# Gram products in four array tiles, T's second layout made on PE, and the first group's 16-to-32 merge as PE products, under a new hand-written order

## The chip, the cores and the metric

The kernel runs on one core of one Trainium2 chip. The metric is the device time of one execution in microseconds (us), lower is better. Before the change the median of three runs is 352.01 us (350.1 to 353.36).

## What is computed

A gated delta rule (linear attention with a correcting state) for 4 x 8 heads, 768 steps, head dimension 48, and behind it a gated convolution layer over the 384 joined features. All data are float32 (the three layer weights arrive as float64 and are converted on the chip).

```python
for t in range(S):
    kt, vt, bt = (k_n[:, :, t], v[:, :, t], beta[:, :, t, None])       # k_n: k divided by its norm
    y[:, :, t] = np.einsum('bhd,bhde->bhe', q[:, :, t], state)
    v_old = np.einsum('bhde,bhd->bhe', state, kt)
    state = state + bt[:, :, :, None] * np.einsum('bhd,bhe->bhde', kt, vt - v_old)
...
for k in range(K):                                                     # K = 5 taps, per feature
    gate_pre += conv_w[k][None, None, :] * xp[:, k:k + S, :]
gate = 1.0 / (1.0 + np.exp(-gate_pre))
val = x @ w_val
return (gate * val @ w_out).astype(np.float32)
```

## The kernel before

The 768 steps are cut into 12 chunks of 64, and two chunks form a **group** (6 groups). Inside a chunk the recursion is solved at once: with the Gram matrix of the keys (64 x 64 for each of the 32 heads, 16 pairs of heads side by side), a triangular inverse T turns values into corrected values; only the 48 x 48 state is handed from chunk to chunk.

**Per group, `prep(g)`.** Four loads `KQ` (keys and queries of half a chunk's heads; three buffers). `gram` on PE (TensorE) writes the Gram products of four pairs into a PSUM bank, key against key and query, with a contraction of 48: one head of a pair lies in partitions 64 to 111 and writes output rows 0 to 63, the other lies in 0 to 47 and writes rows 64 to 127. So two 64 x 64 tiles of the array work at once. ACT (ScalarE) copies the bank to `GL`, then the diagonal blocks of 32 to `D1`. DVE (VectorE) transposes them in 32 x 32 blocks (`TL`; this row opens a group's work on DVE), works out the coefficients (`coef`, 18 small rows), and inverts each block of 32: `row` up to size 8, `mergez8` and `merget8` from 8 to 16, and **`zmul`/`zred`/`tmul`/`tred` from 16 to 32**. Part of those products runs on POOL (GpSimd): two of eight in the first group (whose six others are on DVE), four in the later ones. `D1` is their scratch, so the next group's diagonal copies wait until they are done. Last, DVE transposes the result **twice** (`trans_out`): into `TTR`, and in the other layout into `TNA`. From 32 to 64 the step is on PE: `lev1` (tile `z`), a copy to `ZS`, `lev2` (tile `t`, with `TNA` as the stationary side), and a copy into `BD`, the full T of a chunk.

**Per chunk, `chain(ch)`**: products `e` (state by keys), `u` (T by values) and `SPS` (state update), with `eevac` on DVE between `e` and `u` and copies on ACT; then `y`, whose result goes to `YS` and `X`, and six small DMAs (`X<-YS`) that lay the features out.

**Per chunk, `moe(ch)`**: two of five taps as PE products (`conv`), three on DVE (`tap`, in PSUM), the sigmoid on ACT, `val` on PE, `gate` on DVE, `out` on PE, and the stores.

PSUM has 8 banks: 2 for the state, 3 in a pool "c" (chain, conv, y), 3 in a pool "w" (gram, z, t, val, out).

**Order.** Each helper is an entry of a plan with its engine. The table `ORDER` lists the entries by number, and each engine runs its own entries in that order, strictly one after another, waiting on semaphores; entries of -1 are `keep_warm` products of zeros on PE. SP (SyncE) issues all loads in its own part of that order. The weights pass through two staging slots: a load, ACT and DVE rows on the bits (`f64_bits`, four rows on DVE), a copy, and two POOL rows (`f64_join`); the next load of a slot waits for them.

## Time and profile before

| | |
|---|---|
| median of 3 runs | 352.01 us (350.1 to 353.36) |
| the profiled execution | 352.4 us, span 350.7 us |
| PE busy | 318.4 us (91%), of which products of zeros (L758) 32.9 us |
| DVE busy | 260.8 us (74%) |
| ACT busy | 194.3 us (55%) |
| POOL busy | 123.0 us (35%) |
| mean granted PE clock | 0.946 |

The profiled execution is 0.1% above the median. A row of a view names the line, the engine, the operation, the tile written and the tiles read, with shapes. PE records a float32 product twice, so 32 products of `gram` appear as 64 records; matmuls overlap in the array, so a record's own duration is longer than the step from one to the next. `PEclk` is the granted clock of PE as a share of full speed.

### The profile page before, as it was taken

Reading aid. Unit: us, or ns where it says so; the run is one execution under the profiler, and the core shown is the slowest. Engines: PE = TensorE matmul, PEld = TensorE weight load, DVE = VectorE, ACT = ScalarE, POOL = GpSimd, SP = SyncE. Lnnn points to the kernel's source line nnn. Section 1 sums busy time; section 2 is a strip of 40 time slices with the busy share of each in tenths; the row PEclk is TensorE's granted clock in tenths of the full one; section 3 lists DMA queues with packets and bytes.
Section 4 is the critical chain, followed back from the end, with each engine's and each line's share of the span. In section 5 each row is a group of like instructions: output and inputs, shape, how many; then the busy total and the mean of one; then the engine's idle time right before and its main releaser. Section 6 shows DMA issues by size and latency. Waiting matters only on the chain.

```text
span 350.7 us, 13815 instructions
## 1 busy us (share of the span) xinstructions
PE 318.4 (91%) x5998; PEld 262.1 (75%) x5998; DVE 260.8 (74%) x565; ACT 194.3 (55%) x428; POOL 123.0 (35%) x92
## 2 busy tenths in 40 slices
PE   8769997689299799999799999999988999999994
PEld 5768997689288687878668778777677787687872
DVE  5038999999789876999956999789885689612550
ACT  6643400898149853379764797447973421974221
POOL 6425047034891026512068400545204564000000
PEclk9985899668769999999999999999999999999999
DMA  7999711036274534144574435135253332101122
GB/s 201 249 269 277 190 52 47 7 104 187 67 170 133 151 110 118 32 141 126 140 200 119 136 99 152 50 85 158 56 152 104 80 78 49 38 15 36 36 45 45
DMA packets 20283, 39.47 MB, mean 113 GB/s; under 512 B 8112, under 2 KB 11312, under 8 KB 20224
## 3 DMA queue, kind: packets, MB, share of 16 engines
q1 hardware_dynamic: 20224, 38.60, 41.5%
q8 instruction: 47, 0.77, 0.9%
q14 instruction: 12, 0.10, 0.1%
HBM read 32.69 MB, written 4.72 MB: 107 GB/s over the span
## 4 chain that ended last, share of the span: by engine, by line
PE 62%; DVE 21%; ACT 6%; DMA 5%; issue 3%; POOL 1%; SPq 0%; ACTq 0%; DVEq 0%
PE val L704 14%; PE out L715 12%; PE conv L689 9%; PE gram L351 6%; DMA KQ<-in_kq_dram 5%; PE e L570 5%; PE u L570 3%; PE SPS L570 3%; PE y L638 3%; PE y L640 2%; DVE PR L426 2%; DVE TT__83 L433 2%; PE z L450 2%; PE t L470 2%; ACT D L214 2%
## 5 line engine op out<-in xcount | busy, mean ns | idle before, releaser
L694 DVE SCALAR_TENSOR_TENSOR conv<-X,CW,conv 128x256 f32<-128x256 f32 x108 | 48.5, 486 | 19.7 <-PE conv L689 12.8
L351 PE MATMUL gram<-KQ 48*64 48x128 f32 x768 | 54.0, 295 | 6.1 <-DMA KQ<-in_kq_dram 5.6
L704 PE MATMUL val<-X,WV 128*128 128x256 f32 x216 | 53.4, 388 | 1.3 <-ACT GL L214 1.3
L351 PEld LDWEIGHTS gram<-KQ 48*64 48x64 f32 x768 | 47.7, 147 | 8.5 <-issue 3.5
L715 PE MATMUL out<-WO,GT 128*128 128x384 f32 x144 | 50.3, 490 | 0.0
L704 PEld LDWEIGHTS val<-X,WV 128*128 128x128 f32 x216 | 39.5, 189 | 8.5 <-ACT GL L214 1.4
L214 ACT ACTIVATE GL<-gram 128x512 f32<-128x512 f32 x48 | 28.1, 596 | 23.1 <-PE gram L351 22.7
L689 PE MATMUL conv<-X,DW 128*128 128x256 f32 x144 | 37.9, 399 | 0.5 <-DMA X<-YS 0.5
L715 PEld LDWEIGHTS out<-WO,GT 128*128 128x128 f32 x144 | 26.8, 189 | 15.0 <-issue 0.2
L570 PE MATMUL u<-VT,BD 64*64 64x48 f32 x768 | 31.1, 230 | 7.2 <-DVE VT L622 6.2
L570 PEld LDWEIGHTS u<-VT,BD 64*64 64x64 f32 x768 | 27.3, 144 | 10.7 <-issue 8.7
L548 POOL TENSOR_SCALAR_AFFINE_SELECT AQ<-GL 64x1024 f32<-64x1024 f32 x24 | 28.3, 1180 | 16.5 <-PE y L638 12.2
L214 ACT ACTIVATE D<-GL 32x512 f32<-32x512 f32 (+1 forms) x36 | 22.7, 631 | 19.7 <-DVE TT__83 L433 19.1
L758 PEld LDWEIGHTS SPS<-ZW 128*128 128x128 f32 x242 | 31.3, 210 | 2.8 <-issue 2.7
L758 PE MATMUL SPS<-ZW 128*128 128x128 f32 x242 | 32.9, 298 | 0.0
L708 DVE TENSOR_TENSOR GT<-val,GT 128x256 f32<-128x256 f32 x36 | 15.0, 420 | 20.8 <-PE val L704 18.8
L689 PEld LDWEIGHTS conv<-X,DW 128*128 128x128 f32 x144 | 26.2, 193 | 5.1 <-issue 0.6
L342 POOL TENSOR_TENSOR VT<-VT,NRM 128x768 f32<-128x768 f32 x12 | 17.7, 1477 | 35.1 <-DMA VT<-in_vt_dram 27.7
L638 PE MATMUL y<-AQ,US 112*64 112x64 f32 x384 | 29.1, 233 | 0.0
L638 PEld LDWEIGHTS y<-AQ,US 112*64 112x64 f32 x384 | 25.9, 146 | 3.6 <-issue 2.2
L698 ACT ACTIVATE GT<-conv 128x256 f32<-128x256 f32 x36 | 13.4, 387 | 27.1 <-DVE conv L694 27.0
L640 PE MATMUL y<-AQ,US 128*48 128x64 f32 x384 | 28.0, 230 | 0.0
(97 smaller groups left out, 591.2 us busy)
## 6 DMA issues: line engine op xcount, KB each, us to landing
KQ<-in_kq_dram SPq DMA_DIRECT2D x24, 448.0 KB, 4.7
KF<-in_kf_dram SPq DMA_DIRECT2D x11, 448.0 KB, 3.9
VT<-in_vt_dram SPq DMA_DIRECT2D x12, 384.0 KB, 4.1
AQ<-in_qf_dram SPq DMA_DIRECT2D x24, 192.0 KB, 3.6
KT<-in_kt_dram SPq DMA_DIRECT2D x12, 384.0 KB, 3.5
out_dram<-OS SPq DMA_DIRECT2D x48, 96.0 KB, 2.2
AQ<-in_w_val_dram SPq DMA_DIRECT2D x3, 384.0 KB, 11.0
AQ<-in_w_out_dram SPq DMA_DIRECT2D x3, 384.0 KB, 12.7
```

The source lines that it names most:

```text
L214: A.activation(out=out, in_=in_, func=AF.Copy, **kw)
L342: G.tensor_tensor(out=VT[c], in0=VT[c], in1=NRM[:, c * NP:(c + 1) * NP].unsqueeze(2).to_broadcast([128, NP, D]), op=ALU.mult)
L351: PE.matmul(p[64 * a:64 * a + 64, 128 * j:128 * (j + 1)], x[:, 0:C], x, start=True, stop=True)
L548: G.affine_select(out=AQ[c][r0:r0 + 64, j], in_=GL[r0:r0 + 64, c * NP:(c + 1) * NP, 64:128], pattern=[[0, NP], [1, C]], compare_op=ALU.is_ ...
L570: return lambda: PE.matmul(*a, stop=True, **k)
L638: PE.matmul(p[0:64, C * j:C * j + C], US[ch % 3][0:112, 0, h, D * j:D * j + 64], AQ[c][0:112, 0, pp, :], start=True, stop=True)
L640: PE.matmul(p[64:112, C * j:C * j + C], us[:, 1, h, j, :], AQ[c][:, 1, pp, :], start=True, stop=True)
L689: PE.matmul(p[:, 0:B * C].rearrange("p (b t) -> p b t", t=C), DW[:, m, i, :], x[:, m, :, k:k + C], start=(i == 0), stop=(i == len(PTAPS) - 1))
L694: V.scalar_tensor_tensor(out=p, in0=x[:, m, :, k:k + C], scalar=CW[:, m, k:k + 1], in1=p, op0=ALU.mult, op1=ALU.add)
L704: PE.matmul(p[:, 0:B * C].rearrange("p (b t) -> p b t", t=C), WV[:, k, 128 * m:128 * m + 128], xs[:, k], start=(k == 0), stop=(k == NKT - 1))
L715: PE.matmul(bank["o", ch, i][:, 0:DM], GT[k][:, 2 * i:2 * i + 2, :].rearrange("p b t -> p (b t)"), WO[:, k, :], start=(k == 0), stop=(k == ...
L758: PE.matmul(SPS[0][:, 384:512], ZW, ZW, start=False, stop=True, skip_group_check=True)
```

## The change

1. **Gram in four tiles.** The host swaps the two partition halves for the upper four pairs of each `KQ` load. `gram` now takes a whole load at once, eight pairs into two banks, and goes round the four 64 x 64 tiles. There are 24 calls of 16 products instead of 48 of 8; each holds two of the three "w" banks. The number of products (384) and their size are the same.
2. **T's layout on PE.** The second DVE transpose goes in groups 1 to 5. Instead `lev0` multiplies `TTR` by the identity `EYE` (tile `n`, 32 products a chunk), and ACT copies it to `TN`. `z`, `n` and `t` now lie in four strips of 32 partitions that match, so `zevac` is one copy of 128 partitions instead of four of 32; `lev2` uses four tiles of the array on its diagonal.
3. **The first group's merge on PE** (`MERGE = (0,)`): `TTR` and `TNA` are transposed with the two blocks of 16 still apart; `mergew` (128 products of 32x16), a DVE row `mergew_evac` into `WI`, `mergeq` (128 more) and an ACT copy into `TTR` supply the missing corner. The 16 rows of zmul to tred of group 0 (14 on DVE, 2 on POOL) go. The later groups keep theirs.
4. Small: `halves` (16 short POOL rows at the start, for the constants `IDH` and `ML`); `PTAPS` unchanged, the new branches on it don't act.
5. **A new `ORDER`**: every engine's rows move; `keep_warm` goes from 121 products to 53.

```diff
+MERGE = (0,)
 ORDER = [
-    1, 4, 8, 2, 16, 110, 5, 160, 3, 65, 162, 6, 70, 9, 10, 7, 11, 12, 13, 161, 0, 14, 75, 15, 17, 24, 64, 18, 19,
+    -3, 66, 9, 17, 67, 71, 76, 151, 10, 68, 11, 12, 13, 14, 15, 72, 18, 2, 0, 6, 16, 19, 20, 21, 22, 25, 81, 69, 70,
...
+        def gram_bank(c, h):
+            bank["g", g, c, 2 * h] = wps("gram")
+
         def gram(c, h):
-            p = bank["g", g, c, h] = wps("gram")
-            kq_ = KQ[(4 * g + 2 * c + h // 2) % 3]
+            bank["g", g, c, 2 * h + 1] = wps("gram")
+            kq_ = KQ[(4 * g + 2 * c + h) % 3]
             for j in range(QB):
-                for a, r in ((0, slice(64, 112)), (1, slice(0, D))):
-                    x = kq_[r, QB * (h % 2) + j, :]
-                    PE.matmul(p[64 * a:64 * a + 64, 128 * j:128 * (j + 1)], x[:, 0:C], x, start=True, stop=True)
+                for a in range(2):
+                    for s in range(2):
+                        r = 64 * (a ^ s ^ 1)
+                        x = kq_[r:r + D, QB * s + j, :]
+                        PE.matmul(bank["g", g, c, 2 * h + s][64 * a:64 * a + 64, 128 * j:128 * (j + 1)], x[:, 0:C], x,
+                                  start=True, stop=True)
...
+        def mergew(c):
+            for u in range(c * NP, (c + 1) * NP):
+                for r in range(0, 128, 32):
+                    PE.matmul(bank["mw", g][r:r + 32, 16 * u:16 * u + 16], GL[r:r + 32, u, r % 64:r % 64 + 32],
+                              TTR[r:r + 32, u, 16:32], start=True, stop=True, tile_position=(r, r))
+        def mergew_evac():
+            V.scalar_tensor_tensor(
+                out=WI, in0=bank["mw", g].rearrange("p (u x) -> p u x", x=16), scalar=ML[:, 0:1],
+                in1=IDH.unsqueeze(1).to_broadcast([128, NU, 16]), op0=ALU.mult, op1=ALU.add)
+        def mergeq(c):
...
+                    PE.matmul(bank["mq", g][r:r + 32, 16 * u:16 * u + 16], TNA[r:r + 32, u, :], WI[r:r + 32, u, :],
+                              start=True, stop=True, tile_position=(r, r))
+        def mergeq_evac():
+            copy(A, TTR[:, :, 16:32], bank["mq", g].rearrange("p (u x) -> p u x", x=16))
+        def lev0(c):
+            p = bank["n", g, c] = wps("n")
+            for pp in range(NP):
                 u, x = c * NP + pp, 32 * (pp // 2)
                 for r in (0, 64):
-                    to = r + 32 * (pp % 2)
+                    to = 64 * (pp % 2) + r // 2
+                    PE.matmul(p[to:to + 32, x:x + 32], TTR[r:r + 32, u, :], EYE[r:r + 32, r:r + 32],
+                              start=True, stop=True, tile_position=(r, to))
+        def nevac(c):
+            copy(A, TN, bank["n", g, c][:, 0:256].rearrange("p (u x) -> p u x", x=32))
...
-                    PE.matmul(p[to:to + 32, x:x + 32], TNA[r:r + 32, u, :], ZS[r:r + 32, pp, :],
-                              start=True, stop=True, tile_position=(r, to))
+                    PE.matmul(p[to:to + 32, 32 * x:32 * x + 32], TN[to:to + 32, x, :], ZS[to:to + 32, x, :],
+                              start=True, stop=True, tile_position=(to, to))
...
+        if g in MERGE:
+            add("DVE", 1.15, trans_out, (0,), r=["TT"], w=["TTR"])
+            add("DVE", 1.15, trans_out, (1,), r=["TT"], w=["TNA"], kind="trans_nat")
...
-        add("DVE", 1.15, trans_out, (1,), r=["TT"], w=["TNA"])
...
+    kq[:, :, 0:D, QB:], kq[:, :, 64:112, QB:] = kq[:, :, 64:112, QB:].copy(), kq[:, :, 0:D, QB:].copy()
```

The new order shows at three places. First SP, which issues the loads, from the start of the program. Before, the fourth `KQ` load (the second time `KQ0` stands) is the 13th load; the rows are loads 2 to 13:

```order
L219 DMA AQ1_79<-in_w_val_dram 128x768
L219 DMA VT1_75<-in_vt_dram 128x768
L219 DMA KQ0_67<-in_kq_dram 112x1024
L219 DMA AQ0_78<-in_qf_dram 48x1024
L219 DMA KQ1_68<-in_kq_dram 112x1024
L219 DMA BE_108<-in_beta_dram 128x192
L219 DMA AQ0_78<-in_qf_dram 48x1024
L219 DMA KQ2_69<-in_kq_dram 112x1024
L219 DMA AQ1_79<-in_w_val_dram 128x768
L219 DMA KF1_77<-in_kf_dram 112x1024
L219 DMA VT0_74<-in_vt_dram 128x768
L219 DMA KQ0_67<-in_kq_dram 112x1024
```

With the change, SP's loads 1 to 10:

```order
L223 DMA KQ0_67<-in_kq_dram 112x1024
L223 DMA AQ1_79<-in_conv_w_dram 128x30
L223 DMA AQ1_79<-in_w_val_dram 128x768
L223 DMA KQ1_68<-in_kq_dram 112x1024
L223 DMA KQ2_69<-in_kq_dram 112x1024
L223 DMA AQ1_79<-in_w_val_dram 128x768
L223 DMA KQ0_67<-in_kq_dram 112x1024
L223 DMA VT1_75<-in_vt_dram 128x768
L223 DMA BE_108<-in_beta_dram 128x192
L223 DMA AQ1_79<-in_w_val_dram 128x768
```

The fourth `KQ` is now the seventh load, and the loads of `qf`, `kf` and the other values stand behind the third part of `w_val`.

Second DVE, where group 0's inverse ends. Before, the last rows of the merge (L426 and L433), then both transposes, then the first row of group 1 (L364); the rows on AQ1 belong to the weights:

```order
L426 TENSOR_TENSOR PR<-ZT,TT__83 128x512
L433 TENSOR_REDUCE TT__83<-PR 128x16x4
L426 TENSOR_TENSOR PR<-ZT,TT__83 128x768
L433 TENSOR_REDUCE TT__83<-PR 128x16x4
L273 TENSOR_SCALAR AQ_79<-AQ_79 128x384
L433 TENSOR_REDUCE TT__83<-D_86 128x16x4
L275 TENSOR_SCALAR AQ_79<-AQ_79 128x384
L438 STREAM_TRANSPOSE TTR<-TT__83 128x32x32
L440 STREAM_TRANSPOSE TNA<-TT__83 128x32x32
L277 SCALAR_TENSOR_TENSOR AQ_79<-AQ_79 128x384
L364 STREAM_TRANSPOSE TLP<-D_86 128x32x32
```

With the change the same place (L422 and L427 are the last rows from 8 to 16; ROOT, NRM and QUOT are coefficients, of group 1 here):

```order
L422 TENSOR_TENSOR PR<-ZT,TT__83 128x256 x2
L427 TENSOR_REDUCE TT__83<-PR 128x2x8x4
L341 TENSOR_TENSOR ROOT<-SS,ROOT 128x32
L293 TENSOR_SCALAR X_99<-X_99 128x384
L343 TENSOR_SCALAR ROOT<-ROOT 128x32
L457 STREAM_TRANSPOSE TTR<-TT__83 128x32x32
L345 STREAM_TRANSPOSE NRM_110<-ROOT 128x32
L459 STREAM_TRANSPOSE TNA<-TT__83 128x32x32
L347 TENSOR_TENSOR QUOT<-ROOT 128x32
L349 RECIPROCAL QUOT<-QUOT 128x32
L470 SCALAR_TENSOR_TENSOR WI<-mw,ML,IDH 128x512
```

Group 1's first transpose and most of its coefficients have moved ahead of group 0's `TTR`, and the 16-to-32 rows of group 0 are gone.

Third PE between the last early `gram` and the first chunk's `u`. Before:

```order
L351 MATMUL gram<-KQ_68 64x128 x16
L758 MATMUL SPS_120<-ZW 128x128 x73
L450 MATMUL z<-TTR,GL_80 32x32 x32
L351 MATMUL gram<-KQ_69 64x128 x16
L351 MATMUL gram<-KQ_67 64x128 x16
L470 MATMUL t_675<-ZS,TNA 32x32 x32
```

With the change:

```order
L369 MATMUL gram<-KQ_68 64x128 x16
L824 MATMUL SPS_124<-ZW 128x128 x48
L466 MATMUL mw<-TTR,GL_80 32x16 x128
L824 MATMUL SPS_124<-ZW 128x128 x2
L479 MATMUL mq<-WI,TNA 32x16 x128
L491 MATMUL n<-EYE,TTR 32x32 x32
L503 MATMUL z<-TTR,GL_80 32x32 x32
L369 MATMUL gram<-KQ_69 64x128 x16
L519 MATMUL t_918<-ZS,TN 32x32 x32
```

Fewer products of zeros stand ahead, and `mw`, `mq` and `n` stand between `TTR` and `z`.

## The prediction

> **What bounds the kernel now.** I read first the busy time of the engines by stage, cut at rows of DVE that the whole program waits for: the first transpose of group 0 (26.58), the ends of `TTR` of groups 0, 1 and 5 (64.24, 108.58, 298.25), and the last copy of `out` (346.2). Columns: stage, length, busy us of PE, its weight loads, DVE, ACT, POOL, then granted clock.

> ```profile
> 0.00:26.58 26.58, 20.10 (x184) 16.33 (x184) 8.31 (x25) 15.51 (x30) 11.63 (x17) 0.94 0.95 240
> 26.58:64.24 37.66, 32.74 (x302) 31.11 (x302) 36.01 (x68) 8.75 (x16) 15.06 (x8) 0.86 0.48 130
> 64.24:108.58 44.34, 36.81 (x892) 33.39 (x892) 39.61 (x73) 30.33 (x64) 25.09 (x17) 0.73 0.41 112
> 108.58:298.25 189.67, 181.41 (x3823) 145.62 (x3824) 158.06 (x362) 115.86 (x264) 71.00 (x49) 1.00 0.42 113
> 298.25:346.20 47.95, 47.31 (x799) 35.63 (x797) 18.78 (x40) 23.36 (x57) 0.22 (x1) 1.00 0.14 31
> ```

> Three regimes. Until 26.58 the DMA engines set the pace (share 0.95). Until 108.58 it is DVE (75.6 of 82.0 us; PE's busy time there holds most of its products of zeros). From 108.58 it is PE: 8.3 us idle of 189.67, then 0.6 of 47.95, while DVE has 31.6 us to spare. So work taken from DVE shortens the second regime in full and the third only through waits; work taken from PE shortens the third.

> **First regime.** The chain of waits and the rows of time show what starts DVE's row at 26.58.

> ```profile
> 10.99 0.31 SPq L219 DMA_DIRECT2D KQ<-in_kq_dram  x1
> 21.85 2.10 PE L351 MATMUL gram<-KQ 48*64 48x128 f32 x32 [2.73 <-DMA KQ<-in_kq_dram]
> 24.04 0.36 DVE L273 TENSOR_SCALAR AQ<-AQ 128x384 f32<-128x384 f32 x1 [4.06 <-ACT AQ L271]
> 24.61 1.93 ACT L214 ACTIVATE D<-GL 128x512 f32<-128x512 f32 x3
> 26.58 2.08 DVE L364 STREAM_TRANSPOSE TLP<-D 128x1024 f32<-128x1024 f32 x1 [0.73 <-ACT D L214]
> KQ<-in_kq_dram SPq DMA_DIRECT2D x7, 448.0 KB, 10.7
> AQ<-in_w_val_dram SPq DMA_DIRECT2D x3, 384.0 KB, 11.0
> BE<-in_beta_dram SPq DMA_DIRECT2D x1, 96.0 KB, 8.0
> AQ<-in_conv_w_dram SPq DMA_DIRECT2D x1, 15.0 KB, 1.9
> VT<-in_vt_dram SPq DMA_DIRECT2D x2, 384.0 KB, 7.5
> KF<-in_kf_dram SPq DMA_DIRECT2D x2, 448.0 KB, 12.9
> AQ<-in_qf_dram SPq DMA_DIRECT2D x2, 192.0 KB, 7.4
> 0.81 0.40 SPq L219 DMA_DIRECT2D AQ<-in_conv_w_dram  x1
> ```

> By the order of SP, 4271 KB are issued up to and with the fourth `KQ` (15, two w_val, two VT, KF, BE, two qf, four KQ); they have landed 21.04 us after the first issue, 203 KB a microsecond. In the new order 2575 KB stand up to the fourth `KQ`: 0.81 + 12.7 = 13.5; its gram (1.0), two copies to `GL` (1.2) and the diagonal (1.93) end at 17.6. But DVE must first pass four rows on the third part of `w_val`, which lands after 3439 KB, at 17.8; ACT's row and the four of DVE (0.55 and 1.66, as at 23.47 to 25.8) make 20.0. So DVE starts at 20.0 instead of 26.58: **-6.6 us** (bounds: 17.6 if the weights come earlier; 26.58 if the queue's waits keep the old pace).

> **Second regime.** Of DVE's 82.0 us this goes:

> ```profile
> 45.10 0.96 DVE L413 TENSOR_TENSOR PR<-TLP,TT__83 128x768 f32<-128x768 f32 x1
> 49.48 0.35 DVE L273 TENSOR_SCALAR X<-X 128x384 f32<-128x384 f32 x1
> 61.93 0.35 DVE L275 TENSOR_SCALAR AQ<-AQ 128x384 uint32<-128x384 uint32 x1
> 62.20 2.04 DVE L438 STREAM_TRANSPOSE TTR<-TT__83 128x1024 f32<-128x1024 f32 x1
> 101.73 0.49 DVE L694 SCALAR_TENSOR_TENSOR conv<-X,CW,conv 128x256 f32<-128x256 f32 x1 [1.26 <-issue]
> 104.70 1.99 DVE L440 STREAM_TRANSPOSE TNA<-TT__83 128x1024 f32<-128x1024 f32 x1
> 106.52 2.06 DVE L438 STREAM_TRANSPOSE TTR<-TT__83 128x1024 f32<-128x1024 f32 x1
> ```

> The merge of group 0 fills 45.10 to 62.20, 17.1 us, less six rows on the weights in it (the first and last are shown; 2.3 us), which stay: 14.8. Group 1's `TNA`: 1.8 (start to start). Two taps stand ahead of group 1's `TTR` now and behind it in the new order: 1.0, and the wait of 1.26 ahead of the first goes with them. Together 18.9. The weights' rows in the stage are twelve in both orders, so they cancel.

> Added: `WI` on DVE, 512 elements from PSUM, which no row has. Between one tap (0.49 for 256, the row above) and two: 0.9. It waits for `mw`, 128 products. The nearest rows are `t` and `z`, 32x32, in 64 records:

> ```profile
> 42.98 16.57 PE L758 MATMUL SPS<-ZW 128*128 128x128 f32 x146
> 64.38 1.03 PE L450 MATMUL z<-TTR,GL 32*32 32x32 f32 x64 [4.83 <-DVE TTR L438]
> 65.34 4.96 PE L351 MATMUL gram<-KQ 48*64 48x128 f32 x44
> 302.81 0.75 PE L470 MATMUL t<-ZS,TNA 32*32 32x32 f32 x64
> 303.49 1.56 PE L704 MATMUL val<-X,WV 128*128 128x256 f32 x6
> 8.99 1.96 PE L351 MATMUL gram<-KQ 48*64 48x128 f32 x32 [0.82 <-DMA KQ<-in_kq_dram]
> ```

> From start to start `t` takes 0.68 (10.6 ns a record), `z` after an idle PE 0.96 (15 ns). `mw` and `mq` have 256 records each, at about the slow rate since PE has idled: 4.1 us (2.7 to 7.4, the latter at 29 ns, the step of `e` alone, quoted below). DVE has 2.7 us of rows meanwhile (`TNA`, three small ones), so it stalls 1.4. The stage becomes 82.0 - 18.9 + 0.9 + 1.4 = 65.4: **-16.6 us**. `TTR` of group 1 ends at 85.4 instead of 108.58.

> Is PE ready there? `TTR` of group 0 ends about 50.5; `mw`, `WI`, `mq`, and a copy of some 0.6 make about 60.2, so `z` of chunk 0 comes at 61.5 (64.38 before), late only by the two PE trips. From there the chain of chunks 0 and 1 has some 20 us of PE work and as many ACT copies; adding the rows one behind another, I get the first conv at 84, three of 0.87, and PE free at 86.6, about when DVE is. I take no further loss, with 0 to 8 as bounds. The 48 zeros ahead of `mw` are 96 records; at the pace of the row at 42.98 (146 in 16.6) they take 10.9. The `KQ` load ahead of them is the eighth, behind 6767 KB, so 34; with its gram they end about 46, before `TTR` at 50.5, and nothing waits for them.

> The clock speaks against this part. At 64.38 PE had idled 4.83 us, and the gram behind it takes 113 ns a record against 61 at 8.99; the stage ran at 0.73. The change issues 68 fewer zeros. If everything from 61 to 86 went at half speed, the 20 us of work that is not bound by small products would take 40. [...]

> **Third regime.** From group 1's first `z` to the end the orders hold the same products of chain, conv, val and out within two or three; of gram 192 remain in both. These go through four tiles instead of two. Two tiles: 16 records in 0.945 (32 in 1.89 in the chain of waits), 59 ns a record. Four tiles have a near relative, `e` and `u` interleaved:

> ```profile
> 109.09 1.89 PE gram L351 x32
> 131.00 0.93 PE e L570 x32
> 144.43 0.87 PE conv L689 x4
> 147.10 0.26 PE L570 MATMUL e<-US,KF 48*64 48x48 f32 x2
> 148.38 1.56 PE L704 MATMUL val<-X,WV 128*128 128x256 f32 x6
> ```

> 64 records in 1.28 us, 20 ns each, though `e` alone in two tiles steps by 29. Per product gram is wider (128 against 48), so 59/2 = 29.5 is my value; bounds 20 and 59. 384 records: 22.7 us become 11.3, -11.3 (-15 to 0).

> [...]

> `n` adds 320 products there, 640 records at 10.6 to 15 ns: +6.8 to +9.6, I take 7.5 (at 29 ns 19). Its copies are ACT's, which gains: four `ZS` copies become one. So PE: **-3.8 us**.

> ```profile
> L440 DVE STREAM_TRANSPOSE TNA<-TT__83 128x1024 f32<-128x1024 f32 x6 | 11.9, 1986 | 0.1
> L214 ACT ACTIVATE ZS<-z 32x256 f32<-32x256 f32 x48 | 18.0, 374 | 1.8 <-PE z L450 0.8
> 346.17 0.49 ACT L214 ACTIVATE OS<-out 128x384 f32<-128x384 f32 x1 [0.80 <-PE out L715]
> ```

> DVE loses four `TNA` there, 8 us. PE's waits on it can shrink by at most the 8.3 us of idle time; I take **-3** (0 to -8). The tail behind 346.17, 4.5 us of copy and store, stays.

> **Sum**, against the profiled execution (352.4 us, span 350.7, 0.1% over the median): 352.4 - 6.6 - 16.6 - 3.8 - 3 = **322.4, forecast 322**.

> **Rivals.**
> 1. *Gram gains nothing from four tiles* (bank or weight port): PE keeps the 11.3, so 334. For: PE's weight loads are busy 145.6 of 189.7 us. Against: 20 ns of `e` and `u`, whose weights are as wide.
> 2. *The start stays cold or waits on PE's two trips.* Between 61 and 86 at 0.73 the 20 us become 27: 329. At half speed 342. For: the row at 65.34. Against: DVE, not PE, set that stage.
> 3. *PE and DVE fit better than before*: the whole 8.3 of idle time goes, and `n` runs at 10.6 ns: 316; with gram at 20 ns 313.
> 4. *Slower: the "w" banks run out.* Gram takes two of three at once and needs both free; until ACT has copied them, `val` and `out` have one. The longest such wait now is small:

> ```profile
> PE val L704 <- ACT GL L214: 1.3, 1, 1.3
> ```

> To turn 322 into more than 355.5, each of the 12 gram calls of the third regime would have to cost 2.8 us in waits (12 x 2.8 = 34); at 3 us 358. Against: two copies last 1.2 us, and ACT is busy 61% there.
> 5. *The new order just moves the idle time*: DVE's 23.2 us are spent in other waits and only PE's part is left, 349 to 351. For: DVE is idle 31.6 us in the third regime already.

> **How the numbers follow.** Forecast (314 to 328) 0.48, rival 1 0.12, rival 2 0.17, rival 3 0.13, rival 4 0.05, rival 5 0.05. About 1% is what a measurement of this kernel tells from no change. Faster: the first four, 0.90; same 0.05; slower 0.05. The range leaves out rivals 4 and 5 and the far end of 2. Its high end is rival 1 with `n` some 4 us dearer; its low end is rival 3 with a start at 17.6 and the faster `mw` and `mq` (2.4 and 2.8 off 313): 308 to 338.

> **What would show it.** DVE's first transpose near 20; `TTR` of group 0 near 50 and of group 1 near 85; `mw` and `mq` about 4 us each; gram near 30 ns a record; `n` about 0.8 a call; PE idle under 5% behind group 1's `TTR`; no waits over 1 us on `GL` copies. The forecast is wrong if the fourth `KQ` still lands past 18, if `z` of group 1 comes long after its `TTR`, or if gram still steps by 50 ns or more.

## The result: slower, 365.1 us against 352.7

The changed kernel takes 365.14 us (median of 4 runs, 362.42 to 366.9), the kernel before 352.65 (350.1 to 353.36): ratio 1.036, 95% interval 1.028 to 1.045. The forecast was 322. The profiled execution took 366.9 us (span 365.2), at a mean granted PE clock of 0.855 against 0.946. Ratios, here and below, leave out executions that are over 1.5% above the fastest of the same kernel and compare with the kernel before as it ran beside each run; medians and ranges are of all executions.

The busy time by stage, cut at the same events as before the change: DVE's first transpose, the ends of `TTR` of groups 0, 1 and 5, the last copy of `out`. Columns as above: stage, length, PE, its weight loads, DVE, ACT, POOL, granted clock, DMA share, GB/s.

```profile
0.00:20.54 20.54, 11.96 (x158) 8.61 (x162) 11.03 (x24) 15.02 (x30) 11.93 (x32) 0.77 0.89 256
20.54:47.36 26.82, 20.19 (x212) 18.49 (x204) 25.58 (x78) 10.77 (x20) 7.32 (x7) 0.73 0.54 157
47.36:100.20 52.84, 38.23 (x1508) 35.60 (x1508) 27.73 (x49) 24.43 (x53) 22.01 (x14) 0.61 0.33 94
100.20:310.21 210.01, 193.01 (x4318) 153.31 (x4319) 154.90 (x361) 110.81 (x249) 72.48 (x50) 0.91 0.40 110
310.21:360.80 50.59, 49.25 (x955) 38.46 (x953) 18.07 (x40) 22.29 (x54) 3.93 (x4) 0.97 0.15 34
```

| event, us | before | forecast | after |
|---|---|---|---|
| DVE's first transpose | 26.58 | 20.0 | 20.54 |
| end of `TTR`, group 0 | 64.24 | 50.5 | 47.36 |
| end of `TTR`, group 1 | 108.58 | 85.4 | 100.20 |
| from there to `TTR`, group 5 | 189.67 | 182.9 | 210.01 |
| from there to the last copy of `out` | 47.95 | 47.95 | 50.59 |

The start came as forecast, group 0's `TTR` even 3 us earlier. From there to the last copy of `out` the kernel before needs 282.0 us (64.24 to 346.20); the forecast gave 265.8, the changed kernel needs 313.4. Of the 44.5 us between the forecast's sum (322.4) and the profiled execution (366.9) the third regime holds 27.1, the second 14.3, the tail 2.6, the start 0.5. In the third, PE's idle time is 17.0 us where the forecast left 5.3 (8.3 less 3), and its busy time 193.0 where it had 177.6 (181.4 less 3.8), at a clock of 0.91 instead of 1.00.

What PE does in the first of these stretches, from the view of its rows in order of time (start, busy us, what it did, records; in brackets the idle time ahead of it and what ended it):

```profile
47.50 2.85 PE L466 MATMUL mw<-TTR,GL 32*32 32x16 f32 x242 [3.97 <-DVE TTR L457]
51.80 0.41 PE L466 MATMUL mw<-TTR,GL 32*32 32x16 f32 x14 [1.45 <-issue]
52.14 1.22 PE L824 MATMUL SPS<-ZW 128*128 128x128 f32 x4
53.29 1.68 PE L479 MATMUL mq<-WI,TNA 32*32 32x16 f32 x109
58.45 1.90 PE L479 MATMUL mq<-WI,TNA 32*32 32x16 f32 x128 [3.48 <-issue]
62.19 0.50 PE L479 MATMUL mq<-WI,TNA 32*32 32x16 f32 x19 [1.84 <-issue]
```

`mq` runs 109 records, waits 3.48 us, runs 128, waits 1.84, runs 19. The 14 records of `mw`, 4 of zeros and 109 of `mq` between two pauses are 127, one short of 128 (between them, at 53.06, the trace also has a semaphore instruction of PE, which isn't a record). "issue" means that no semaphore or transfer which the profile shows ended the wait. PE has two instructions a record, a weight load and a matmul (7142 of each on the page), so 128 records are 256 instructions. The DMA queues say what comes in that measure; the row of the queue that carries instructions, before and after:

```profile
q8 instruction: 47, 0.77, 0.9%
```

```profile
q8 instruction: 56, 0.92, 1.1%
```

0.92 MB in 56 packets are 16.4 KB each, and 0.92 MB for PE's 14284 instructions 64 bytes each: a packet would hold 256 of them, and 14284 make 55.8 packets (before 11996 make 46.9). So by an estimate from these counts PE's program comes in blocks of 256 instructions, and it comes while PE runs (the first of the 56 packets begins at 15.86 us, the last at 344.96). The times of these packets in the trace fit: those that begin at 49.43, 55.93 and 59.62 us are followed by the ends of the three pauses above, 2.4 to 2.6 us later, and each of the changed kernel's pauses on issue ends 2.2 to 3.1 us behind the start of such a packet. The list of PE's waits (engine, line, what it waited for: us in total, times, longest) has such waits on issue all over the kernel, 18 in all, most of them at the small products or just behind them:

```profile
PE gram L369 <- DMA KQ<-in_kq_dram: 9.1, 5, 3.9
PE z L503 <- issue: 6.4, 5, 2.6
PE mq L479 <- issue: 5.3, 2, 3.5
PE SPS L631 <- issue: 5.1, 5, 1.8
PE mw L466 <- DVE TTR L457: 4.0, 1, 4.0
PE t L519 <- issue: 3.8, 2, 2.3
PE conv L753 <- DMA X<-YS: 3.3, 2, 2.6
PE conv L753 <- issue: 2.7, 1, 2.7
PE u L631 <- issue: 2.0, 1, 2.0
PE mw L466 <- issue: 1.4, 1, 1.4
PE gram L369 <- ACT GL L218: 1.2, 3, 0.7
```

All rows on issue, those left out here too, add up to 27.3 us; before the change to 5.4, with these as the largest:

```profile
PE SPS L570 <- issue: 2.1, 2, 1.9
PE t L470 <- issue: 1.6, 2, 1.5
```

So the mark was in the profile before: `t`, behind a bunch of `z`, waited 1.5 us for nothing named.

### The profile page after: what moved, and what is told of

Read it like the earlier page. It is cut to its first block, busy times and chain, and to the rows that moved or that the text cites. A ratio compares the mean times of both kernels' runs of the same rounds, so it can differ in the third digit from the quotient of the medians.

```text
span 365.2 us, 16025 instructions
## 1 busy us (share of the span) xinstructions
PE 312.6 (86%) x7142; PEld 254.5 (70%) x7142; DVE 237.3 (65%) x547; ACT 183.8 (50%) x405; POOL 117.7 (32%) x106
## 2 busy tenths in 40 slices
DMA packets 20292, 39.61 MB, mean 108 GB/s; under 512 B 8112, under 2 KB 11312, under 8 KB 20224
## 4 chain that ended last, share of the span: by engine, by line
PE 72%; issue 8%; DVE 8%; ACT 5%; DMA 4%; SPq 2%; ACTq 0%; DVEq 0%
PE val L767 16%; PE out L778 12%; PE conv L753 10%; PE gram L369 6%; PE e L631 5%; PE y L699 3%; PE u L631 3%; PE SPS L631 3%; PE y L701 3%; PE z L503 3%; PE t L519 3%; DMA X<-YS 2%; PE n L491 2%; SPq L223 2%; DMA AQ<-in_w_val_dram 1%
## 5 line engine op out<-in xcount | busy, mean ns | idle before, releaser
L757 DVE SCALAR_TENSOR_TENSOR conv<-X,CW,conv 128x256 f32<-128x256 f32 x108 | 50.4, 483 | 33.4 <-PE conv L753 17.6
L767 PE MATMUL val<-X,WV 128*128 128x256 f32 x216 | 60.5, 430 | 0.0
L767 PEld LDWEIGHTS val<-X,WV 128*128 128x128 f32 x216 | 45.0, 214 | 9.2 <-issue 0.3
L369 PE MATMUL gram<-KQ 48*64 48x128 f32 x768 | 39.0, 353 | 10.3 <-DMA KQ<-in_kq_dram 9.1
L753 PE MATMUL conv<-X,DW 128*128 128x256 f32 x144 | 39.8, 414 | 6.0 <-DMA X<-YS 3.3
L369 PEld LDWEIGHTS gram<-KQ 48*64 48x64 f32 x768 | 31.2, 179 | 16.2 <-issue 6.6
L683 DVE TENSOR_TENSOR VT<-e,VT 128x384 f32<-128x384 f32 x22 | 12.2, 556 | 44.6 <-PE e L631 29.3
L432 POOL TENSOR_TENSOR PR<-TLP,TT__83 128x768 f32<-128x768 f32 x5 | 11.1, 2217 | 84.9 <-DVE TT__83 L427 55.4
L355 POOL TENSOR_TENSOR VT<-VT,NRM 128x768 f32<-128x768 f32 x12 | 17.7, 1477 | 61.3 <-DMA VT<-in_vt_dram 42.2
L778 PEld LDWEIGHTS out<-WO,GT 128*128 128x128 f32 x144 | 26.6, 189 | 14.8 <-issue 0.2
L631 PE MATMUL SPS<-US,KT 64*48 64x48 f32 x704 | 24.1, 216 | 5.1 <-issue 5.1
L631 PEld LDWEIGHTS e<-US,KF 48*64 48x64 f32 x704 | 25.1, 143 | 3.4 <-issue 1.8
## 6 DMA issues: line engine op xcount, KB each, us to landing
KQ<-in_kq_dram SPq DMA_DIRECT2D x24, 448.0 KB, 4.8
KF<-in_kf_dram SPq DMA_DIRECT2D x11, 448.0 KB, 4.1
VT<-in_vt_dram SPq DMA_DIRECT2D x12, 384.0 KB, 5.2
KT<-in_kt_dram SPq DMA_DIRECT2D x12, 384.0 KB, 3.9
AQ<-in_qf_dram SPq DMA_DIRECT2D x24, 192.0 KB, 3.4
AQ<-in_w_val_dram SPq DMA_DIRECT2D x3, 384.0 KB, 5.2
AQ<-in_w_out_dram SPq DMA_DIRECT2D x3, 384.0 KB, 3.7
```

Of the source, the lines that this page charges most:

```text
L355: G.tensor_tensor(out=VT[c], in0=VT[c], in1=NRM[:, c * NP:(c + 1) * NP].unsqueeze(2).to_broadcast([128, NP, D]), op=ALU.mult)
L369: PE.matmul(bank["g", g, c, 2 * h + s][64 * a:64 * a + 64, 128 * j:128 * (j + 1)], x[:, 0:C], x, start=True, stop=True)
L631: return lambda: PE.matmul(*a, stop=True, **k)
L753: PE.matmul(p, DW[:, m, i, :], x[:, m, :, k:k + C], start=(i == 0), stop=(i == len(PTAPS) - 1))
L757: V.scalar_tensor_tensor(out=p, in0=x[:, m, :, k:k + C], scalar=CW[:, m, k:k + 1], in1=p, op0=ALU.mult, op1=ALU.add)
L767: PE.matmul(p[:, 0:B * C].rearrange("p (b t) -> p b t", t=C), WV[:, k, 128 * m:128 * m + 128], xs[:, k], start=(k == 0), stop=(k == NKT - 1))
```

## The experiments

The theories. **A**: PE's program arrives in blocks of 256 instructions, one per some 3.6 us, and bunches of small products outrun it ("A alone": and nothing else costs). **B**: the half clock comes from the 68 products of zeros that the new order leaves out. **C**: the new order is itself late (loads of `KQ`, `X`). **D**: taking two "w" banks at a time starves the others. **E**: four dense tiles cost by themselves. **F**: a pause costs twice, by the half clock behind it. **G**: DVE's queue is in the wrong order.

| run | us, median (range) | ratio to before, 95% interval |
|---|---|---|
| e1 n as one product | 340.98 (336.61 to 342.89) | 0.974, 0.966 to 0.982 |
| e2 mw, mq as wide products | 353.64 (347.03 to 356.62) | 0.995, 0.987 to 1.002 |
| e5 both | 336.89 (333.46 to 337.89) | 0.959, 0.951 to 0.968 |
| e6 layout by DVE again | 351.62 (347.38 to 357.34) | 0.998, 0.992 to 1.004 |
| e7 and no merge on PE | 353.60 (348.32 to 363.77) | 0.999, 0.993 to 1.005 |
| e9 n in wide transposes | 352.27 (350.15 to 368.12) | 1.002, 0.998 to 1.006 |
| e3 before with the four-tile gram | 366.11 (363.11 to 367.65) | 1.041, 1.032 to 1.050 |
| e10 the same, two tiles | 359.13 (351.04 to 362.75) | none |
| e4 changed, two-tile gram | 367.41 (360.53 to 368.29) | none |
| e14 e3 with 28 zeros | 369.72 (363.43 to 372.23) | none |
| e8 changed, 70 more zeros | 375.93 (372.5 to 377.29) | 1.069, 1.059 to 1.080 |
| e12 changed, 41 zeros late | 367.20 (362.87 to 368.26) | 1.041, 1.031 to 1.052 |
| e13 changed, 105 zeros | 368.32 (360.78 to 369.57) | none |
| e15 changed, DVE's order | 365.02 (364.11 to 367.11) | 1.032, 1.026 to 1.039 |
| e16 layout by DVE, DVE's order | 343.13 (340.39 to 348.16) | 0.968, 0.962 to 0.974 |

"None" stands where the executions gave no interval.

### The rate of PE's program (e11)

```diff
+def small(i, n):
+    for k in range(n):
+        r, x = 32 * (k % 4), 16 * (k // 4 % 32)
+        PE.matmul(PH[i][r:r + 32, x:x + 16], XS[i][r:r + 32, 0:32], XS[i][r:r + 32, 32:48],
+                  start=True, stop=True, tile_position=(r, r))
...
+    small(0, 576)
```

> A kernel of nothing but streams of products, each behind about 30 us in which PE waits: 576 of 32x32 by 16 in four tiles, 576 of 64x64 by 48 in two tiles, 256 of 128x128 by 64, 128 of 128x128 by 256, and the first stream again while 7 MB are loaded. Each product is two records and four instructions. Its output isn't the reference's. Theory A: the first stream runs at PE's own pace (7 to 15 ns a record) for one or two blocks, then pauses at every 128 records; 128 records take 3.4 to 4.1 us each, so its 1152 records take 30 to 36 us instead of 8 to 17; 64x64 by 48 is bound the same way or just not (28 to 32 ns a record); the two wide streams show no pauses. With loads beside it a block takes as long or longer. Rival: there is no such limit; the first stream holds 7 to 15 ns a record to its end.

The first stream, PE's rows in order of time:

```profile
19.39 3.18 PE L69 MATMUL PH<-XS 32*32 32x16 f32 x223 [19.39 <-DVE XS L64]
23.98 1.90 PE L69 MATMUL PH<-XS 32*32 32x16 f32 x128 [1.41 <-issue]
27.43 1.90 PE L69 MATMUL PH<-XS 32*32 32x16 f32 x128 [1.55 <-issue]
31.16 1.90 PE L69 MATMUL PH<-XS 32*32 32x16 f32 x128 [1.83 <-issue]
34.89 1.90 PE L69 MATMUL PH<-XS 32*32 32x16 f32 x128 [1.83 <-issue]
38.62 1.90 PE L69 MATMUL PH<-XS 32*32 32x16 f32 x128 [1.83 <-issue]
42.34 1.90 PE L69 MATMUL PH<-XS 32*32 32x16 f32 x128 [1.83 <-issue]
45.80 1.90 PE L69 MATMUL PH<-XS 32*32 32x16 f32 x128 [1.56 <-issue]
49.25 0.62 PE L69 MATMUL PH<-XS 32*32 32x16 f32 x33 [1.56 <-issue]
```

After a long wait 223 records run without a pause, then exactly 128 at a time. From 23.98 to 49.25 are seven blocks, 3.61 us each: 28 ns a record, of which PE uses about half. Its own pace shows within a block, 128 records in 1.90 us. The second stream, 64x64 by 48, has no pause:

```profile
L75 PE MATMUL PH<-XS 64*64 64x48 f32 x1152 | 36.2, 225 | 24.1 <-DVE XS L64 24.1
```

36.2 us for 1152 records are 31 ns a record, just over the block's pace. The 128x128 streams had none either (256 and 512 records in 58.0 and 109.5 us). The loads that were to run beside the last stream were over before it began, so their influence wasn't measured. What the clock does to such a bunch shows in the changed kernel: 118 records of `mw` start in the 0.99 us from 47.50 to 48.49, where the clock fell, and 128 of `mq` (58.45) take 1.90 us at a clock of 0.50. So a bunch fits into the block's 3.6 us at half clock too. Theory A's rate is shown. A pause at a block took 1.4 to 1.8 us in this stream; in the changed kernel the waits on issue took 0.3 to 3.5 us each, 27.3 us at 18 of its 56 blocks.

### Fewer instructions, the same order (e1, e2, e5)

e1 replaces 32 products a chunk by one, which leaves out the transposition; e2 the 64 of `mw` and of `mq` a chunk by one each, with one block's weights for all; e5 has both:

```diff
-            for pp in range(NP):
...
-                    PE.matmul(p[to:to + 32, x:x + 32], TTR[r:r + 32, u, :], EYE[r:r + 32, r:r + 32],
-                              start=True, stop=True, tile_position=(r, to))
+            PE.matmul(p[:, 0:256], EYE, TTR[:, c * NP:c * NP + HB, :].rearrange("p u k -> p (u k)"), start=True, stop=True)
```

```diff
-            for u in range(c * NP, (c + 1) * NP):
...
-                              TTR[r:r + 32, u, 16:32], start=True, stop=True, tile_position=(r, r))
+            PE.matmul(bank["mw", g][:, 256 * c:256 * c + 256].rearrange("p (u x) -> p u x", x=16),
+                      GL[:, c * NP, :], TTR[:, c * NP:(c + 1) * NP, 16:32], start=True, stop=True)
```

> The changed kernel, but n (the layout of T for the last product) is made by one product of 128x128 by 256 per chunk instead of 32 of 32x32 by 32, with EYE as the weights, so that T stands there not transposed: the values are not the reference's, the order and everything else are as in the changed kernel. 744 of 7142 PE records go (1488 of 14284 instructions). Theory A, PE's program arrives in blocks of 256 instructions, one per about 3.6 us, and bunches of small products outrun it: 5.8 blocks fewer, in the bunches; the pauses at n, z and t shrink, the clock stays up longer behind them; 345 to 355 us, mean clock 0.88 or more. Theory B, the half clock comes from the 68 products by zeros that the new order leaves out: same as the changed kernel, 361 to 366. Theory C, the new order itself is late (KQ and X loads): 361 to 366.

> The changed kernel, but the two products of the first group's merge, mw and mq, are made by one wide product per chunk each (4 products instead of 256 of 32x32 by 16), so the values are not the reference's; the order, the banks and the evictions are as in the changed kernel. 504 of 7142 PE records go, all between 47 and 63 us. Theory A (blocks of code): 4 blocks of 3.6 us fewer there; mq ends at 54 to 57 instead of 62.7, the second group's TTR is ready 6 to 10 us earlier than 100.2, and the time is 353 to 360. Theory B (zeros) and theory C (order, loads): the merge is 3 to 4 us shorter by its own products' time, the half clock from 48.5 to 89.5 stays, 361 to 364.

> The changed kernel with both edits of the two lean runs at once: n by one wide product a chunk, and mw and mq by one wide product a chunk each; the values are not the reference's, the order is the changed kernel's. Theory A (PE's program arrives in blocks of 256 instructions, 3.6 us apart, and a pause throws the clock to half): the two gains add, 365 less 24 less 11.5, so 326 to 334, mean clock 0.92 or more; that is near the time that was forecast for the change, with its products costing what the forecast took for them. Theory B or C: the two overlap or stop at something else, 338 to 345.

e1 takes 24 us off the changed kernel's time (22 by the ratios), more than A's 345 to 355 gave. PE's own time for `n` is not what was saved: the products keep PE busy for 10.8 us in the changed kernel, the wide ones for 9.1. 5.8 blocks fewer make some 4 us a block. B and C would have left 361 to 366; both fall for `n`. The profiled executions, 30.3 us apart in span, show two parts. PE's idle time is 13.6 us less (11.1 of that on issue), and its busy time 16.7 us less: 1.7 of that is `n`, and for the rest the same products run faster, `val` alone in 52.4 instead of 60.5 us. The stages of e1 (`TTR` of group 1 to that of group 5, and on to the last copy):

```profile
96.27:281.80 185.53, 177.04 (x3813) 139.72 (x3813) 155.16 (x361) 110.24 (x249) 70.83 (x48) 0.99 0.45 122
281.80:330.50 48.70, 47.66 (x831) 37.07 (x829) 18.02 (x40) 22.06 (x54) 3.93 (x4) 1.00 0.17 40
```

The third regime falls from 210.0 to 185.5 us, close to the 182.9 forecast, and the clock is back at 0.99 with no product of zeros added. e2 takes 11.5 us off (15 by the ratios): its median of 353.6 is at the low end of A's 353 to 360, and its executions begin at 347.0. Group 1's `TTR` ends at 88.4, 11.8 us earlier where A gave 6 to 10. Here the clock can't be the reason: from group 0's `TTR` to that of group 1 the stage takes 41.3 us instead of 52.8 at a clock of 0.63 instead of 0.61, and the waits on issue in it are 0.5 us instead of 10.8 (the products' own busy time falls by 3.6). The two together do not add: 336.9, where A had said 326 to 334. e5's stages show why:

```profile
46.12:85.70 39.58, 34.13 (x890) 29.39 (x891) 28.70 (x50) 24.43 (x53) 24.29 (x17) 0.74 0.45 127
85.70:278.90 193.20, 180.92 (x3813) 142.27 (x3812) 154.61 (x361) 110.18 (x249) 70.65 (x48) 0.97 0.43 116
278.90:330.50 51.60, 49.90 (x831) 38.84 (x829) 18.11 (x41) 22.31 (x54) 3.93 (x4) 0.93 0.17 40
```

Group 1's `TTR` ends at 85.70, where 85.4 was forecast, 10.6 us earlier than in e1; but the last copy of `out` is at 330.50 in both profiled executions. What is gained there is given back behind it: the same 3813 and 831 records take 7.7 and 2.9 us longer than in e1, 4.5 us of that PE's idle time and 6.1 its busy time, at clocks of 0.97 and 0.93 instead of 0.99 and 1.00. Why the clock falls there in e5 and not in e1 is open.

### Is it the clock? (e8, e12, e13)

The edits are entries of -1 in the order, ahead of the entry named (group, chunk; a number in front is how many):

```diff
 e8:  +6 behind mergew (0, 1), +8 behind mergeq (0, 1), +4 behind each lev1 of group 0, +8 ahead of lev1 (1, 0),
      +4 ahead of lev1 (2..5, 0), +3 behind the second gram of each chunk of groups 2 to 5
 e12: +10 lev1 (1, 1), +7 lev2 (2, 0), +9 lev2 (3, 0), +9 lev0 (4, 1), +6 lev2 (5, 0)
 e13: as e12, and of group 0 +16 mergew 0, +4 mergew 1, +10 mergeq 0, +10 mergeq 1, +6 lev1 0, +4 lev2 0, +6 lev1 1, +8 usmul 0
```

> The changed kernel with 70 more products by zeros (123 in all, as many as the kernel before has), put where PE pauses: between mw and mq, behind mq, behind z of the first group, ahead of z and behind the gram of each later group. Theory B (the half clock comes from the zeros that were left out): mean clock 0.92 or more instead of 0.855, and 345 to 357. Theory A: a zero behind a block boundary waits for the same code, and 280 more instructions are one more block; the pauses stay, 362 to 371.

> The changed kernel with 41 more products by zeros at five places behind 89.5 us (10, 7, 9, 9, 6 of them), each just ahead of the bunch of small products in whose middle PE paused 1.3 to 3.2 us at a block of its program and the clock fell to half for the next 3 to 14 us (41 us in all). In a block whose successor isn't there yet the zeros take time in which PE would only wait. Theory F (a pause costs twice: itself and the half clock behind it): the five half-clock stretches go or shrink to under 15 us, mean clock 0.90 or more, and the time is 346 to 358 although 41 products and 164 instructions are added. Theory A alone (the blocks set the time, the clock is only a sign): 364 to 370.

> The run with 41 late zeros, with 64 more of them between 43 and 78 us: 16 while PE waits for the first TTR, 4 to 10 at each pause of mw, mq, n, z, t, u (64 zeros are two records each, so just one block more, and the later places stay where they are in their blocks). Theory F: the half clock from 48.5 to 89.5 us shrinks by half or more, mean clock 0.93 or more, the second group's TTR is ready 3 to 8 us earlier than in the run with the late zeros alone, and the time 3 to 8 us less. Theory A: one block and some more code in the stretch that code sets: 3 to 6 us more than that run.

The granted clock, per fortieth of the span, in the changed kernel and then in e8:

```profile
PEclk9555965556995799986999969999988999989999
```

```profile
PEclk9555966988995899995799998999999999999999
```

The clock rose in all three, from 0.855 to 0.894 (e8), 0.891 (e12) and 0.924 (e13, profiled executions). The time did not fall: 376 (above what either theory gave), 367 (as A gave), 368 (1 us more than e12, where A gave 3 to 6 more and F as much less). Zeros don't win the time back: B falls, and so does what F forecast of them, 346 to 358 for e12. But the half clock is not free. `val` in the kernel before, the changed kernel and e12:

```profile
L704 PE MATMUL val<-X,WV 128*128 128x256 f32 x216 | 53.4, 388 | 1.3 <-ACT GL L214 1.3
L767 PE MATMUL val<-X,WV 128*128 128x256 f32 x216 | 60.5, 430 | 0.0
L768 PE MATMUL val<-X,WV 128*128 128x256 f32 x216 | 55.3, 401 | 1.9 <-issue 1.9
```

The same products take 7.1 us more in the changed kernel than before, and 5.2 less again with e12's zeros. PE's busy time is 312.6 us in the changed kernel and 312.9 in e12: `keep_warm` takes 12.6 us more of it (27.7 for 15.1), all else 12.3 less. In e8 it is 26.0 more (41.1) and 15.4 less. So the zeros cost at least what the clock won, and by these figures the half clock holds some 12 to 15 us of PE's busy time in the changed kernel, perhaps more, since the zeros did not bring the clock up everywhere (an estimate). e13 shows it from `TTR` of group 0 to that of group 1:

```profile
47.90:99.64 51.74, 41.97 (x1606) 38.64 (x1607) 28.28 (x49) 24.43 (x53) 21.82 (x14) 0.93 0.34 93
```

At a clock of 0.93 instead of 0.61 the stage takes 51.7 us instead of 52.8, with PE busy on zeros for 14.4 us of it instead of 1.2; all else keeps PE busy for 9.4 us less. A bunch that waits for blocks has room for the half clock (128 records of `mq` took 1.90 us at 0.50, and a block of the rate kernel 3.61); the wide products beside it lose by it.

### DVE's wait, and where the order put it (e15)

DVE, in order of time, in the changed kernel:

```profile
66.92 1.28 DVE L439 TENSOR_REDUCE ZT<-PR 128x64 f32<-128x256 f32 x2
85.91 0.56 DVE L683 TENSOR_TENSOR VT<-e,VT 128x384 f32<-128x384 f32 x1 [17.72 <-PE e L631]
```

The new order has DVE add `e` of chunk 1 in the middle of group 1's inverse, where PE's `e` was to be ready; it comes 17.7 us later, and the inverse stands behind it. e15 moves the rest of the inverse ahead:

```diff
 zred(g1, 1)
+zred(g1, 0), tmul(g1, 0..3), tred(g1, 0..3), trans_out(g1)
 eevac(chunk 1, 0)
-zred(g1, 0), tmul(g1, 0..3)
 eevac(chunk 1, 1)
...
```

> The changed kernel with one edit of the order: the rest of the second group's inverse on DVE (nine instructions, and two of POOL) stands ahead of the three additions of e (eevac) that DVE waited 17.7, 3.7 and 0.7 us for between 68 and 97 us. Theory G (those waits stood in DVE's queue ahead of the inverse because PE's products were late, and the group's TTR was late for that): TTR of the second group ready at 78 to 88 instead of 100.2 us, its z and t at once behind PE's own work, and 351 to 360 in all. Theory A alone (PE's stream of code sets the time from the first merge on, DVE's wait hides beside it): TTR early, but 362 to 367.

`TTR` of group 1 ends at 86.4 instead of 100.2, and the time is 365.0. A wait of 17.7 us taken away, and nothing won: G falls, and the time is in the 362 to 367 that A alone gave. Even this `TTR` waits for PE, which still reads group 0's in `n`:

```profile
84.29 2.15 DVE L457 STREAM_TRANSPOSE TTR<-TT__83 128x1024 f32<-128x1024 f32 x1 [5.84 <-PE n L491]
```

From 47 us on PE's stream, with its pauses and its clock, sets the time.

### Gram in four tiles (e3, e10, e14, e4)

e3 is before with gram's code, host layout and plan entries as in the diff above, in the order of before (gram where its second half stood, some entries later where no bank was free). e10 and e4 turn the loops:

```diff
-            for j in range(QB):
-                for a in range(2):
-                    for s in range(2):
+            for s in range(2):
+                for j in range(QB):
+                    for a in range(2):
```

e14 is e3 with zeros:

```diff
 e14: +4 lev1 (1, 1), +3 and +3 the grams of (3, 1), +3 lev2 (2, 0), +6 second gram of (4, 0), +3 lev1 (2, 1), +3 lev2 (3, 0), +3 conv of chunk 4
```

> The kernel before with the gram in four tiles alone (two banks at a time, the data laid out for it), in the order of before; no n, no merge by products, no changed zeros. Theory A (blocks of code): gram takes 29 instead of 59 ns a record where its code is there; the number of instructions is as before, so little is lost elsewhere: 342 to 349. Theory D, two of three banks taken at a time starve the others: waits of gram on copies of GL, 352 to 358.

> The changed kernel with the loops of the gram turned so that two tiles run at a time instead of four; banks, data, number of instructions and order as in the changed kernel. Theory A (blocks of code): gram's records take 59 ns again, 30 ns each more on 768, but code is loaded meanwhile; 365 to 374. Theory D (four tiles or the clock suffer by the dense gram): 355 to 362.

> The run of before with the four-tile gram alone, with the loops turned so that two tiles run at a time; banks taken in pairs, data and order as in that run (366). Theory D (taking two banks at a time and putting the gram where both are free costs, not the speed of its products): 360 to 370. Theory E (the dense four-tile bunches cost, by code or clock): back to 350 to 356.

> The run of before with the four-tile gram alone (366), with 28 more products by zeros at eight places where PE waited 0.6 to 1.6 us in the three windows ahead of its late half-clock stretches (114 to 124, 165 to 189, 216 to 230 us). Theory F: these stretches go, mean clock 0.92 or more instead of 0.866, and the time falls to 345 to 355. Theory D (taking two banks at a time is what costs): 364 to 372.

The four tiles do what was forecast of them (a gram of the changed kernel):

```profile
89.86 1.10 PE L369 MATMUL gram<-KQ 48*64 48x128 f32 x32
```

From this row's start to that of the next (`e`, 90.78) are 0.92 us for 32 records, 29 ns each instead of 59. Yet e3 is 4.1% slower than before, worse than both theories gave, and e4 can't be told from the changed kernel. e3's list of PE's waits against that of before:

```profile
PE gram L356 <- DMA KQ<-in_kq_dram: 11.5, 8, 3.0
PE gram L356 <- ACT GL L214: 3.7, 6, 0.8
PE t L476 <- ACT ZS L214: 1.8, 4, 0.6
PE gram L356 <- ACT ZS L214: 1.8, 3, 0.8
```

```profile
PE gram L351 <- DMA KQ<-in_kq_dram: 5.6, 5, 2.7
```

All of PE's waits add up to 39.3 us in e3 and 27.1 before; those on issue to 3.8 and 5.4. So here the code is not the cause. One part is waits for the `KQ` loads and for ACT to copy banks, which are now taken and loaded in pairs, as rival 4 had it, though in shorter waits. The other is the clock: gram keeps PE busy for 42.5 us instead of 54.0, but from `TTR` of group 1 to that of group 5 PE is busy for 191.8 us instead of 181.4, at a clock of 0.88 instead of 1.00. In e10 that stage ran at 1.00 and took 190.2 us, as before, in the execution that was profiled (351.0 us, mean clock 0.94); the other three took 357 to 363 at mean clocks of 0.89 to 0.92. How much of the 4.1% is the pairs and how much the pace of four tiles stays open. e14's zeros raised the clock (0.905 against 0.866) and won nothing: `keep_warm` takes 46.1 us instead of 34.6, and all else on PE 13.2 less. F's forecast fails here too, by the price of the zeros.

### Without n, and without the merge (e6, e7, e9, e16)

```diff
             add("DVE", 1.15, trans_out, (0,), r=["TT"], w=["TTR"])
+            add("DVE", 1.15, trans_out, (1,), r=["TT"], w=["TNA"], kind="trans_nat")
...
+            if g in MERGE:
                 add("PE", 0.6, lev0, (c,), cols=256, r=["TTR", "EYE"], w=["np"], take="w")
```

e7 sets `MERGE = ()` besides, so that group 0 is made as the others are.

> The changed kernel with T's layout made by DVE again in groups 1 to 5 (a transpose of 2 us each), and by PE for the first group alone, whose T is finished by products; z and t laid out as before; merge, four-tile gram and the order stay. 640 fewer PE records. Theory A: nearly what the wide n gave, 341, plus up to 2 us a group where DVE is waited for: 340 to 350. Theory C (the order is at fault): 360 or more.

> The changed kernel with both additions on PE taken back: T's layout by DVE in all groups and the first group's merge by DVE and POOL; what stays of the change is the four-tile gram and the new order. 1152 fewer PE records than the changed kernel (5990 of 7142). Theory A: the merge's 14.8 us on DVE come back at the start, 11.5 us of code for it go: within 5 us of the run with T's layout alone taken back, 342 to 352. Theory C (the new order or the four tiles cost by themselves): 355 or more.

> The changed kernel with T's layout by PE made in four transposes of 128x128 a chunk (weights: four blocks of T side by side, moving: two column groups of EYE) instead of 32 of 32x32; z's two halves go to two banks so that the result stands where the wide transpose puts T; t is copied in eight pieces instead of four. Values as in the reference. 672 of 7142 PE records go. Theory A (blocks of code): like the run with n as one wide product, 341, plus some us for ACT's four extra copies a chunk and for z now behind n: 340 to 349. Theory B or C (zeros, order): 358 to 366.

> The changed kernel without n on PE: T's layout by a DVE transpose in all groups (in the first from the finished TTR), and the order of DVE as in the run that moves the second group's inverse ahead. 768 of 7142 PE records go (six blocks of code); the merge by products, the four-tile gram and the rest of the order stay; the values are the reference's. Theory A with G: the run with T's layout on DVE was 351.6; one block less at the start and the inverse earlier give 336 to 347, faster than the kernel before. Theory A alone: 345 to 352. If neither the code nor the queue matters: 355 or more.

e6 gives `n` back to DVE in groups 1 to 5 (`trans_nat` behind `trans_out`): 351.6, 13.5 us less than the change, a little outside the 340 to 350 expected; its `TTR` of groups 2 to 5 follow one another at e1's pace (51.9, 45.7, 49.7, 45.1 us against 45.8, 44.6, 50.0, 45.2), except for the first step, so what it lost against e1 it lost early. e7 takes the merge back as well: 353.6, also over its 342 to 352; both misses are smaller than the spread of the executions. That the merge on PE saves DVE 14.8 us can't be told in the time, and what is left of the change in e7, four tiles and the new order, is worth nothing against before. e9 makes `n`, transposition included, in four transposes of 128x128 a chunk:

```diff
+            for s in range(NP // 4):
+                u = c * NP + 4 * s
+                PE.matmul(p[:, 64 * s:64 * s + 64].rearrange("p (a k) -> p a k", k=32),
+                          TTR[:, u:u + 4, :].rearrange("p u k -> p (u k)"), e, start=True, stop=True)
```

352.3, 13 us less than the change but 11 over e1 and over the 340 to 349 expected. Its `n` steps by 138 ns a record, 96 of them, 13 us, so it saves code and no time of PE; the rest of what parts it from e1 I have not split.

e16 is e6 with group 0's layout made by DVE too (`trans_again`), so that `n` is off PE altogether, with the merge kept and e15's order of DVE:

```diff
+        def trans_again():
+            V.transpose(out=TNA, in_=TTR)
...
             add("ACT", 0.57, mergeq_evac, r=["mq"], w=["TTR"], give="w")
+            add("DVE", 1.15, trans_again, r=["TTR"], w=["TNA"])
...
-                add("PE", 0.6, lev0, (c,), cols=256, r=["TTR", "EYE"], w=["np"], take="w")
```

and the DVE order of e15: 343.1, ratio 0.968, faster than both kernels and as A with G gave. Against e6 it is 8.5 us (10 by the ratios), of one block less at the start and the order of e15, which are not told apart.

## Why the prediction was wrong

**The step that failed** is the price of a small product. The second regime took `mw` and `mq` at "about the slow rate" of 15 ns a record, bounds to 29, the third took `n` at 10.6 to 15. Those were durations of `t` and `z`, 64 records alone between wide work, with no wait on issue ahead of them. In bunches a record cost its share of a block, 28 ns in e11, wherever the wide work between didn't pay for it. And the sum put what such pauses bring with them at nothing: it took the third regime at a clock of 1.00, with PE's idle time shrinking. There the waits on issue are 15.2 us (5.1 before), and at 0.91 the same `val` products take 46.0 us instead of 40.3. e1, with 24 records of `n` instead of 768, has 6.6 us of these waits and a clock of 0.99.

- *First regime, -6.6*: right. 20.54 for 20.0.
- *Second regime*: the durations of `WI` (0.75 us for 0.9) and of group 0's end were right. `mw` took 4.6 us for 4.1 (which was 16 ns a record, not 15). `mq` took 9.4, beyond the bound of 7.4. But the forecast had also chosen the wrong engine for this stage: after the change DVE no longer sets it. e15 has `TTR` of group 1 at 86.4, as forecast, and the time of the changed kernel.
- *Third regime, gram -11.3*: the mechanism was right, 29 ns a record for 29.5 at full clock, and the sum wrong: gram's rows in this regime keep PE busy for 16.4 us instead of 24.4, and e3, e4 and e7 show no gain from it. In e3 it went into waits for loads and copies and into a lower clock.
- *Third regime, n +7.5*: the records themselves step by 10.4 ns on average, as taken. e1, which leaves out 620 of the 640, is 24.5 us shorter in this stage and 1.9 in the tail, where group 5's stand: 43 ns a record, with the pauses and the clock that follow from them. Even the bound of 29 ns gave 19 us.
- *DVE's relief, -3*: not there; PE is idle for 17.0 us instead of 8.3, and its own stream is what the stage waits for.
- *The clock*: the paragraph that spoke against the second regime had the right sign of the clock (0.61 there), but the pauses cost beside it (e2, at 0.63, is 11.5 us shorter there). Whether a gap between `mw` and `mq` costs the clock by itself was not shown: the clock had fallen at 48.49, behind the 3.97 us for which PE waited for `TTR`. In the windows counted below 0.8 us without a product was once enough.
- *The rivals*: 2 was right that the start stays slow on PE, and was priced by the clock without the code. 4 ends on the side that came, by another mechanism: gram waits 1.2 us for `GL` copies in the changed kernel. No rival had the code, and none the clock in the third regime.

With the code of `n`, `mw` and `mq` out of the way (e5) the same order takes 336.9. The 14 us that still part it from the forecast are the third regime and the tail, 193.2 and 51.6 us for 182.9 and 47.95. In the third regime 7.0 us of that are PE's idle time (12.3 for 5.3) and 3.3 its busy time (180.9 for 177.6); what would take them away is not shown.

## What to carry to other kernels

Count PE's instructions like a resource: in the rate kernel a block of 256 came every 3.61 us, so of its stream of short records (15 ns each within a block) the first 223 ran freely, and what followed was priced by the block and not by its records. Here saving instructions (13.5 us in e6 by another engine, 13 in e9 by a wide transpose) beat saving array time (gram's four tiles, no gain). Waits on "issue" at multiples of 128 records were the mark, and some 5 us of waits on issue stood in the profile of the kernel before. Look at the clock beside them: here part of the price was paid by wide products that ran slower, and products of zeros raised the clock in e8, e12, e13 and e14 and took no time off. And when a wait is removed, ask which queue ends last behind it: 17.7 us of DVE's wait were worth nothing while PE's stream set the time.

## What the runs showed of the hardware

Gram's four tiles have two row tiles writing to different partitions of one bank, and step by 29 ns at full clock (the row at 89.86) against 59 for two tiles, so a shared bank did not keep them from that pace here.
